# One kernel, two ways to feed the argument matmuls: pairs of 64-row matmuls in halves of the array, or single 128-row matmuls against a moving table padded with zeros

## The chip, the core and the metric

The kernel runs on one core of a Trainium2 chip. The metric is the device time of one execution in microseconds (us). The median of the three runs of the kernel before is 384.66 us (382.64 to 384.88). One further execution was recorded by the profiler; the profile, its chain of waits and all the durations quoted here come from that one.

## What is computed

Two branches read the same input `x` (2048 positions, 640 channels, bf16) and are mixed by a gate:

```
g = sigmoid((x * gate_w).sum(-1))
a = attention(x): 32 heads of 20, each position sees 8 keys at distances 0,2,..,14; then @ wo
b = long convolution of x with K, by FFT of length 4096;  K[d,l] = Re sum_n C[d,n]*dt*B[d,n]*exp(dt*A[d,n]*l)
out = g*a + (1-g)*(b + x*Dskip)
```

The change lies in the making of the convolution kernel K: 640 channels, 192 complex states each, 2048 positions.

## The kernel before

The work falls into four stretches. Up to about 40 us the inputs are loaded and the 12 parameter pieces for each channel and state are worked out on VectorE and ScalarE and stored to DRAM (`SSMParams`, tensor `Sprm`). From 24 to about 140 us TensorE does the QKV projection (L328, tile `tb`). From about 55 to 300 us it does the attention in eight slices of 256 positions: logits (L383, with L403 and L411 for the softmax), the weighted sum of the values (L447) and the output projection (L464). K is made between 73 and 267 us, woven in among these; the first FFT step follows (L1195), and from 301 us on the rest of the FFT convolution (`fft_conv`).

K is made by `KGen` in ten chunks `c`. A chunk has 64 channels: 8 in each of 2 halves of each of 4 groups. It goes through these steps:

- `load_L` issues eight small DMAs from SP. They bring the chunk's parameter pieces from `Sprm` into `L`, a tile of 128 rows. Rows 0 to 63 and rows 64 to 127 each hold a separate set (two rows of ones and 48 rows of pieces). There are two such tiles, used in turn, and a chunk's loads wait for the argument matmuls of two chunks before.
- The arguments. For each of three state tiles `u` and two kinds (0: the sine's argument, 304 columns; 1: the exponent's, 2 x 216 columns) a task of TensorE multiplies `L` (stationary) with the constant table `R` (moving) into a PSUM tile `ar`. A chunk has 12 tasks of kind 0 and 6 of kind 1, so there are 120 and 60 in all. For `u` below 2 a task of kind 0 is two matmuls, a task of kind 1 four; each uses 64 rows and 128 columns of the array (line L768), and the two that differ in `g2` sit in the two halves of its rows. For `u` = 2 the states left over from two halves of channels share a tile: each matmul becomes two of 64 rows and 64 columns (L773), four in the four quarters of the array.
- ScalarE turns each `ar` into sines (L785) or exponentials (L787). `ar` has two buffers, so TensorE can be at most two tasks ahead of ScalarE.
- VectorE multiplies sines and exponentials (`products`, L808 to L810).
- `kmm` sums over the states with 256 small matmuls a chunk (L826, 22 columns each): 128 rows by 32 columns of the array for `u` below 2, and 64 by 32 for `u` = 2, where two halves of channels share the rows. VectorE evicts the sum (L1179).

All these tasks, with those of the attention and the first FFT step, are given to a planner (`Plan`). Each has a duration, a due time and its engines; `Plan.order` lists them in a fixed order, and `emit` chains every engine's instructions in that order. So each engine works strictly in the planned order, and a task that waits holds up all that stands behind it on its engine. An argument task is planned at 0.15, 0.15 and 0.30 us (kind 0, `u` = 0, 1, 2) or 0.22, 0.22 and 0.40 us (kind 1), a quarter of a `kmm` at 0.18 or, for `u` = 2, 0.35 us.

Of the kernel before, what the change touches and what calls it, by code (L numbers as in the profile page):

```python
# [14 lines left out]
BF16 = mybir.dt.bfloat16  # L15
I16 = mybir.dt.int16
NPBF = ml_dtypes.bfloat16
# [19 lines left out]
def _attn_consts():  # L37
# [5 lines left out]
    for wp in range(W):  # L43
# [7 lines left out]
            v=[-164.3, -448.6, 45.4, 323.3, 710.0, 789.4, 646.8, 1095.8], g=[10.7, 292.0, -348.6, -469.5, -539.5, 427.8, 247.2, -1193.3, -158.0, -278.7, -66.5],  # L51
# [443 lines left out]
NST = 192  # L495
# [7 lines left out]
NPC = 12  # L503
KI = 32
MS = list(range(8)) + [258, 260, 262, 516, 772, 256, 512, 768, 1024, 1280, 1536, 1792, 2048, 2048]
NM = len(MS)
FIRST = 13
SW = 4 * (KI + 2 * NM)
EW = 4 * (KI + NM)
# [4 lines left out]
def _arg_consts():  # L514


    i = np.arange(KI)
    m = np.array(MS)
    sp = np.zeros((64, 4, KI), np.float32)
    sq = np.zeros((64, 4, 2, NM), np.float32)  # L520
    ep = np.zeros((64, 4, KI), np.float32)
    eq = np.zeros((64, 4, NM), np.float32)
    for qq in range(4):
        r = 2 + qq * NPC
        for j in range(3):
            sp[r + j, qq] = 8.0 * i - 124.0
            sq[r + j, qq] = (m % 256)[None]
            sq[r + 5 + j, qq] = (m // 256)[None]
        for j in range(2):
            ep[r + 3 + j, qq] = 8.0 * i  # L530
            eq[r + 3 + j, qq] = m
            sq[r + 8 + j, qq] = 1.0
            eq[r + 10 + j, qq] = 0.5
    sp[0] = MAGIC; sq[0] = MAGIC
    sp[1] = 8192.0
    sq[1, :, 0] = 24576.0
    sq[1, :, 1] = 8192.0
    rr = np.concatenate([np.concatenate([p, q.reshape(64, 4, -1)], axis=2).reshape(64, -1) for p, q in ((sp, sq), (ep, eq))], axis=1)
    return np.concatenate([rr, rr], axis=0).astype(NPBF)


def _shift_consts():
# [166 lines left out]
class KGen:  # L709
    def __init__(self, cst, pre, tc, prm):  # L710
        self.tc, self.nc, self.prm = tc, tc.nc, prm
        nc = tc.nc
        self.Lb = []
        for i in range(2):
            L = pre.tile([128, 2, 2, 2 * NST], BF16, name=f"L{i}", tag="PHI", bufs=3)
            nc.gpsimd.memset(L[:], 0.0)
            for g2 in range(2):
                nc.gpsimd.memset(L[64 * g2:64 * g2 + 2], 1.0)
            self.Lb.append(L)
        self.R = cst.tile([128, SW + EW], BF16, name="Rarg")  # L720
        nc.gpsimd.dma_start(self.R[:], nc.inline_tensor(_arg_consts(), name="c_rarg").ap())
        self.S12 = cst.tile([128, 2, 128], BF16, name="S12")
        nc.gpsimd.dma_start(self.S12[:], nc.inline_tensor(_shift_consts(), name="c_s12").ap())
# [10 lines left out]
    def load_L(self, c):  # L734
        nc = self.nc
        L = self.Lb[c % 2]
        for g in range(4):
            for v in range(2):
                d0 = 160 * g + 80 * v + 8 * c
                src = self.prm.S[d0:d0 + 8].rearrange("(s q) i n -> (q i) s n", q=4)  # L740
                nc.sync.dma_start(L[64 * (g % 2) + 2:64 * (g % 2) + 2 + 4 * NPC, g // 2, :, NST * v:NST * v + NST], src)

    def plan(self, pl, pa, pk, start, hold, params, opened, fin):
        nc, R = self.nc, self.R
# [4 lines left out]
        for c in range(NCH):  # L749
            d0, dd = start(c), start(c + 1) - start(c)  # L750
            L = self.Lb[c % 2]
# [4 lines left out]
            for kind in (0, 1) if c % 2 == 0 else (1, 0):  # L756
                for u in range(3):
                    ends[u, kind] = []
                    for gp in range(2):
                        for sub in range(2) if kind == 0 else (None,):  # L760
                            def args(_, u=u, kind=kind, gp=gp, sub=sub, b=b, L=L):
                                ar = b["ar"] = pa.tile([128, 2, 512], F32, name="ar")
                                for sb, a0 in ((sub, 0),) if kind == 0 else ((0, 0), (1, EW)):
                                    c0, ncol = ((0, SW), (SW, EW))[kind]
                                    for g2 in range(2):
                                        rows = slice(64 * g2, 64 * g2 + 64)
                                        if u < 2:
                                            nc.tensor.matmul(ar[:, g2, a0:a0 + ncol], L[rows, gp, sb, NST * u:NST * u + 128], R[rows, c0:c0 + ncol],  # L768
                                                             start=True, stop=True, tile_position=(64 * g2, 0))
                                        else:  # L770
                                            m0 = NST * gp + 128
                                            for h in range(2):
                                                nc.tensor.matmul(ar[64 * h:64 * h + 64, g2, a0:a0 + ncol], L[rows, h, sb, m0:m0 + 64], R[rows, c0:c0 + ncol],  # L773
                                                                 start=True, stop=True, tile_position=(64 * g2, 64 * h))
                                b["ar", u, kind, gp, sub] = ar

                            def act(_, u=u, kind=kind, gp=gp, sub=sub, b=b):
                                opened()
                                ar = b.pop(("ar", u, kind, gp, sub))
                                if gp == 0 and not sub:  # L780
                                    b["T", u, kind] = self.ring[kind][self.turn[kind] % len(self.ring[kind])]
                                    self.turn[kind] += 1
                                dst = b["T", u, kind]
                                if kind == 0:
                                    nc.scalar.activation(dst[:, 2 * gp:2 * gp + 2, sub, :], ar[:].bitcast(I16)[:, :, 0:2 * SW:2], ACT.Sin, scale=SCL)  # L785
                                else:
                                    nc.scalar.activation(dst[:, 2 * gp:2 * gp + 2].rearrange("p g s n -> p g (s n)"), ar[:, :, 0:2 * EW], ACT.Exp)  # L787
                            due = d0 + dd * k / 18.0
                            first = not ends[u, kind]
                            a = pl.add(f"arg{c}{kind}{u}{gp}{sub}", "P", ((0.15, 0.15, 0.30), (0.22, 0.22, 0.40))[kind][u], args, deps=[Lt], after=[prevarg] + ([self.moved] if c == HC + 2 else []), acq=["ar"],  # L790
                                       due=due - pr["argl"], eq=(304, 432)[kind])
                            t = pl.add(f"act{c}{kind}{u}{gp}{sub}", "A", (0.62, 0.83)[kind], act, deps=[a], after=[prevact] + (hold if first and kind == 0 and ns == NTR - 1 else []), acq=[("trg", "exq")[kind]] if first else [],
                                       rel=[("ar", a)], due=due, table=("sin", "exp")[kind])
                            if first:
                                held[u, kind] = t
                                ns += kind == 0
                            prevarg, prevact = a, t
                            argt[c].append(a)
                            ends[u, kind].append(t)
                            k += kind + 1  # L800
            for u in range(3):
# [12 lines left out]
                def kmm(_, u=u, b=b, j=0):  # L814
                    if u == 0 and j == 0:
                        b["kps"] = pk.tile([128, 2, 256], F32, name="kps", tag="kb")
                    pt, qq = b["pq", u]
                    kps, started = b["kps"], b["started"]
                    for ql in (2 * j, 2 * j + 1):
                        for v in range(2):  # L820
                            for c2 in ((u,) if u < 2 else (0, 1)):
                                for g in range(4):
                                    r0 = 0 if u < 2 else 64 * (g // 2)
                                    rows = slice(0, 128) if u < 2 else slice(r0, r0 + 64)
                                    k = 8 * (g if u < 2 else 2 * c2 + g % 2) + ql
                                    nc.tensor.matmul(kps[32 * g:32 * g + 32, c2, NM * ql:NM * ql + NM],  # L826
                                                     pt[rows, k, v, :], qq[rows, k, v, :],
                                                     start=(g not in started), stop=(u == 2 and v == 1), skip_group_check=True,
                                                     tile_position=(r0, 32 * g))
                                    started.add(g)  # L830
                due = d0 + dd * (0.55 + 0.16 * u) + pr["dl"][c]
# [442 lines left out]
```

## Time and profile before

| of the profiled execution | |
|---|---|
| its own time | 384.76 us |
| span from the first to the last instruction | 383.0 us |
| granted TensorE clock, mean | 0.950 |
| argument matmuls L768, from 73.4 to 253.8 us | 320, 37.0 us busy |
| argument matmuls L773, from 82.4 to 257.0 us | 320, 19.6 us busy |
| state sums L826, from 105.3 to 266.6 us | 2560, 30.2 us busy |
| sines L785 (both buffers) and exponentials L787 on ScalarE | 59.6 + 15.1 and 50.2 us |
| products L808, L809 and L810 on VectorE (largest groups) | 16.5, 16.5 and 21.3 us |

A row of the profile gives the engine, the line, what is written from what, the shape, the count, and after the bar the busy time and the mean duration of one. A matmul's duration runs from its start to its modelled end and holds some 0.17 us in which its last columns pass through the array; the next matmul may start inside it. The distance between starts therefore tells what a matmul costs TensorE. PE is TensorE, PEld its weight loads, DVE is VectorE, ACT is ScalarE, POOL is GpSimd. PEclk is the granted TensorE clock as a share of full speed. The chain is the list of steps, each released by the one ahead of it, that ends with the last instruction.

### The profile page before, as it was taken

The page shows a single profiled execution, that of the slowest core. Times are in us where ns is not written, and L with a number is a line of the kernel's source. Part 1 is how long each engine was busy: PE and PEld are TensorE (multiplying, and loading weights), DVE is VectorE, ACT ScalarE, POOL GpSimd, SP SyncE. Part 2 cuts the span into 40 slices and gives each one's busy share as a digit, 9 for nine tenths or more (in the row PEclk, how much of TensorE's full clock was granted, in tenths as well). Part 3 has the DMA queues.
Part 4 walks back from the last instruction along what each step waited for, and adds up shares of the span by engine and source line. Part 5 has one row for each costly group of instructions (what it writes and reads, how often), then busy time and mean ns, then how long its engine had stood idle before and what let it go on. Part 6 is the DMA issues. An engine that isn't in the chain of part 4 may idle for free.

```text
span 383.0 us, 11863 instructions
## 1 busy us (share of the span) xinstructions
PE 316.9 (83%) x5102; PEld 191.0 (50%) x5126; DVE 323.0 (84%) x437; ACT 304.1 (79%) x427; POOL 89.3 (23%) x122
## 2 busy tenths in 40 slices
PE   0268999998999979988997699889999899987760
PEld 0144564433445545444454344557777655656760
DVE  4879997669999989889998799999896389999782
ACT  1699884677979889789879698988987798995890
POOL 8930331140211001513653100100010022000053
PEclk9998999999999999999989757999999999998996
DMA  8982878472645233686455850403740199926056
GB/s 266 373 252 94 246 212 256 117 215 86 193 125 157 64 112 95 158 224 188 104 124 134 274 154 2 151 2 101 254 140 34 36 211 244 207 40 222 2 119 159
DMA packets 51529, 58.84 MB, mean 154 GB/s; under 512 B 36244, under 2 KB 43284, under 8 KB 51220
## 3 DMA queue, kind: packets, MB, share of 16 engines
q1 hardware_dynamic: 41492, 28.78, 28.3%
q0 software_dynamic: 8256, 28.69, 25.6%
q8 instruction: 40, 0.66, 0.7%
q10 hardware_dynamic: 1728, 0.61, 0.7%
q14 instruction: 13, 0.11, 0.1%
HBM read 38.29 MB, written 19.77 MB: 152 GB/s over the span
## 4 chain that ended last, share of the span: by engine, by line
PE 51%; ACT 19%; DVE 13%; DMA 9%; issue 5%; SPq 1%; POOL 1%; POOLq 0%; ACTq 0%; DVEq 0%
PE tb L328 13%; PE tb L447 7%; PE ar L768 6%; PE fp L1024 5%; PE tb L464 5%; PE kps L826 4%; PE bp L1195 3%; DMA aim<-in_B_A_im_dram 3%; ACT big L787 3%; ACT sp_u L1027 3%; ACT big L785 3%; PE lg L383 3%; DVE bufA L985 3%; ACT sp_k L1027 3%; PE ar L773 2%
## 5 line engine op out<-in xcount | busy, mean ns | idle before, releaser
L328 PE MATMUL tb<-bufA 128*128 128x512 bf16 x283 | 71.5, 388 | 6.5 <-DVE bufA L492 2.1
L785 ACT ACTIVATE big<-ar 128x608 bf16<-128x608 int16 x96 | 59.6, 677 | 10.2 <-PE ar L768 9.4
L787 ACT ACTIVATE big<-ar 128x864 bf16<-128x864 f32 x60 | 50.2, 897 | 4.1 <-PE ar L768 3.3
L442 DVE TENSOR_TENSOR pv<-vc,asb 128x2048 bf16<-128x2048 bf16 x40 | 47.2, 1219 | 4.3 <-PE tb L447 2.1
L328 PEld LDWEIGHTS <-bufA 128*128 128x128 bf16 x300 | 33.2, 120 | 35.1 <-issue 12.2
L377 DVE TENSOR_TENSOR prod<-qc,kc 128x2048 bf16<-128x2048 bf16 x40 | 47.9, 1219 | 2.7 <-PE lg L383 2.5
L768 PE MATMUL ar<-Rarg,L 64*128 64x304 bf16 (+1 forms) x320 | 37.0, 290 | 5.8 <-ACT big L785 2.4
L447 PE MATMUL tb<-pv,ident 128*128 128x512 bf16 (+1 forms) x185 | 39.1, 348 | 2.5 <-DVE prj L492 1.0
L826 PE MATMUL kps<-qq,pt 128*32 128x22 bf16 (+1 forms) x2560 | 30.2, 175 | 4.6 <-issue 4.2
L1024 PEld LDWEIGHTS <-PHI 128*128 128x128 bf16 x256 | 24.8, 97 | 17.6 <-issue 7.4
L826 PEld LDWEIGHTS <-pt 128*32 128x32 bf16 (+1 forms) x2560 | 23.3, 93 | 17.5 <-issue 12.3
L464 PE MATMUL tb<-wo_sb,oT 128*128 128x320 bf16 x160 | 27.7, 310 | 0.0
L768 PEld LDWEIGHTS <-L 64*128 64x128 bf16 x320 | 13.7, 94 | 27.7 <-issue 25.3
L447 PEld LDWEIGHTS <-ident 128*128 128x128 bf16 x192 | 17.8, 99 | 17.3 <-issue 5.5
L490 ACT ACTIVATE prj<-tb 128x512 bf16<-128x512 f32 x28 | 16.5, 598 | 10.9 <-PE tb L328 9.9
L959 POOL DMA_DIRECT2D PHI<-c_phi x8 | 4.5, 558 | 79.5 <-PE fp L1024 41.7
L773 PE MATMUL ar<-Rarg,L 64*64 64x304 bf16 (+1 forms) x320 | 19.6, 298 | 3.8 <-ACT big L787 1.6
L1027 ACT ACTIVATE sp_k<-fp 128x1280 bf16<-128x1280 f32 x16 | 19.1, 1236 | 3.3 <-PE fp L1024 3.0
L810 DVE TENSOR_TENSOR qq<-big 128x1408 bf16<-128x1408 bf16 x24 | 21.3, 886 | 0.0
L1024 PE MATMUL fp<-bufA,PHI 128*128 128x320 bf16 x128 | 19.1, 298 | 2.3 <-ACT sp_u L1027 1.5
L243 PE MATMUL ar<-ident,xn 128*128 128x128 bf16 x80 | 7.9, 263 | 15.6 <-DMA xn<-in_A_x_dram 14.1
L1024 PE MATMUL fp<-big,PHI 128*128 128x320 bf16 x128 | 19.2, 298 | 1.8 <-ACT sp_k L1027 1.8
(201 smaller groups left out, 633.0 us busy)
## 6 DMA issues: line engine op xcount, KB each, us to landing
asb<-aS SPq DMA_DIRECT2D x8, 512.0 KB, 4.0
PSI<-c_psi SPq DMA_DIRECT2D x8, 512.0 KB, 10.2
PHI<-c_phi POOLq DMA_DIRECT2D x8, 384.0 KB, 6.6
Sprm<-pc SPq DMA_DIRECT2D x12, 240.0 KB, 3.7
L<-Sprm SPq DMA_DIRECT2D x80, 36.0 KB, 2.6
kc<-kS POOLq DMA_DIRECT2D x8, 337.5 KB, 4.7
vc<-vS POOLq DMA_DIRECT2D x8, 337.5 KB, 4.9
xn<-in_A_x_dram SPq DMA_DIRECT2D x4, 640.0 KB, 12.4
```

The lines of the kernel that those rows point to most:

```text
L328: nc.tensor.matmul(ppf, self.wq[:, kt, which * D + e:(which + 1) * D:5], self.xT[:, c0 // 1024, kt, c0 % 1024:c0 % 1024 + SC], start=(kt = ...
L377: nc.vector.tensor_tensor(b[e][:], b["qc"][:, e, :].unsqueeze(1).to_broadcast([128, W, C]), win(b["kc"][:, e, :], 0, W, DIL, C), ALU.mult)
L442: nc.vector.tensor_tensor(b["pv", e][:, :, k, :].rearrange("p w (b t) -> p w b t", t=64), for_e, aw, ALU.mult)
L447: nc.tensor.matmul(b["op", e][:, 0:n, :], ident[:], b["pv", e][:, w, 0:n, :], start=(w == 0), stop=(w == W - 1))
L464: nc.tensor.matmul(apf[:, :320], b["oT"][:, e, i * 128:(i + 1) * 128], wo_sb[:, e, hf * 320:(hf + 1) * 320], start=(e == 0), stop=(e == 4))
L768: nc.tensor.matmul(ar[:, g2, a0:a0 + ncol], L[rows, gp, sb, NST * u:NST * u + 128], R[rows, c0:c0 + ncol], start=True, stop=True, tile_pos ...
L773: nc.tensor.matmul(ar[64 * h:64 * h + 64, g2, a0:a0 + ncol], L[rows, h, sb, m0:m0 + 64], R[rows, c0:c0 + ncol], start=True, stop=True, til ...
L785: nc.scalar.activation(dst[:, 2 * gp:2 * gp + 2, sub, :], ar[:].bitcast(I16)[:, :, 0:2 * SW:2], ACT.Sin, scale=SCL)
L787: nc.scalar.activation(dst[:, 2 * gp:2 * gp + 2].rearrange("p g s n -> p g (s n)"), ar[:, :, 0:2 * EW], ACT.Exp)
L826: nc.tensor.matmul(kps[32 * g:32 * g + 32, c2, NM * ql:NM * ql + NM], pt[rows, k, v, :], qq[rows, k, v, :], start=(g not in started), stop ...
L1024: nc.tensor.matmul(fp[:, fl, 0:320].rearrange("p (c x) -> p c x", x=32), PHI[:, fl, kind, :], B[:, :, 2 * f1 + ri].rearrange("p c q g -> p ...
L1027: nc.scalar.activation(t[:], fp[:, :, 0:320].rearrange("p f (x g) -> p x f g", g=4), ACT.Identity)
```

## The change

The table `R` is stored twice: once with zeros in rows 64 to 127, once with zeros in rows 0 to 63. Each argument matmul takes all 128 rows of `L` and picks the copy of `R` that has zeros where the other set of rows lies. It no longer names a place in the array. The three state tiles are cut differently out of 384 columns of `L` (two times 192 states): tiles 0 and 2 each belong to one half of the channels, tile 1 holds 64 states of each. Every argument task of kind 0 is then two matmuls of 128 by 128 with 304 columns, every one of kind 1 four with 216. In `kmm` it is now tile 1 that is done in 64-row matmuls and tile 2 in 128-row ones. `load_L` still issues eight DMAs of the same size, in another order and to other columns. The planner's durations and due times are as before.

```diff
@@ _arg_consts
-    return np.concatenate([rr, rr], axis=0).astype(NPBF)
+    z = np.zeros_like(rr)
+    return np.stack([np.concatenate([rr, z], axis=0), np.concatenate([z, rr], axis=0)], axis=1).astype(NPBF)
@@ KGen.__init__
-        self.R = cst.tile([128, SW + EW], BF16, name="Rarg")
+        self.R = cst.tile([128, 2, SW + EW], BF16, name="Rarg")
@@ KGen.load_L
-        for g in range(4):
+        for g in range(2):
             for v in range(2):
-                d0 = 160 * g + 80 * v + 8 * c
-                src = self.prm.S[d0:d0 + 8].rearrange("(s q) i n -> (q i) s n", q=4)
-                nc.sync.dma_start(L[64 * (g % 2) + 2:64 * (g % 2) + 2 + 4 * NPC, g // 2, :, NST * v:NST * v + NST], src)
+                for h in range(2):
+                    d0 = 160 * ((2 * v + g + 2 * h) % 4) + 80 * h + 8 * c
+                    src = self.prm.S[d0:d0 + 8].rearrange("(s q) i n -> (q i) s n", q=4)
+                    l0 = NST * (h ^ v)
+                    nc.sync.dma_start(L[64 * g + 2:64 * g + 2 + 4 * NPC, :, v, l0:l0 + NST], src)
@@ KGen.plan, args
                                     for g2 in range(2):
-                                        rows = slice(64 * g2, 64 * g2 + 64)
-                                        if u < 2:
-                                            nc.tensor.matmul(ar[:, g2, a0:a0 + ncol], L[rows, gp, sb, NST * u:NST * u + 128], R[rows, c0:c0 + ncol],
-                                                             start=True, stop=True, tile_position=(64 * g2, 0))
-                                        else:
-                                            m0 = NST * gp + 128
-                                            for h in range(2):
-                                                nc.tensor.matmul(ar[64 * h:64 * h + 64, g2, a0:a0 + ncol], L[rows, h, sb, m0:m0 + 64], R[rows, c0:c0 + ncol],
-                                                                 start=True, stop=True, tile_position=(64 * g2, 64 * h))
+                                        l0 = 128 * (2 - u if gp else u)
+                                        nc.tensor.matmul(ar[:, g2, a0:a0 + ncol], L[:, sb, gp, l0:l0 + 128], R[:, g2, c0:c0 + ncol],
+                                                         start=True, stop=True)
@@ KGen.plan, kmm
-                            for c2 in ((u,) if u < 2 else (0, 1)):
+                            for h in (0, 1) if u == 1 else (u // 2,):
                                 for g in range(4):
-                                    r0 = 0 if u < 2 else 64 * (g // 2)
-                                    rows = slice(0, 128) if u < 2 else slice(r0, r0 + 64)
-                                    k = 8 * (g if u < 2 else 2 * c2 + g % 2) + ql
-                                    nc.tensor.matmul(kps[32 * g:32 * g + 32, c2, NM * ql:NM * ql + NM],
+                                    r0 = 64 * (g // 2) if u == 1 else 0
+                                    rows = slice(r0, r0 + 64) if u == 1 else slice(0, 128)
+                                    k = 8 * ((g + 2 * h) % 4) + ql
+                                    nc.tensor.matmul(kps[32 * g:32 * g + 32, h, NM * ql:NM * ql + NM],
                                                      pt[rows, k, v, :], qq[rows, k, v, :],
-                                                     start=(g not in started), stop=(u == 2 and v == 1), skip_group_check=True,
+                                                     start=(g not in started), stop=(v == 1 and u == 1 + h), skip_group_check=True,
                                                      tile_position=(r0, 32 * g))
```

## The prediction

> **What bounds the kernel now.** I read the page first (sections 1, 2 and 4), then the groups by shape, the timeline of TensorE, the stretches of 5 us, and last the chain of waits piece by piece from 70 to 260 us, where the changed matmuls lie.
>
> ```profile
> PE 316.9 (83%) x5102; PEld 191.0 (50%) x5126; DVE 323.0 (84%) x437; ACT 304.1 (79%) x427; POOL 89.3 (23%) x122
> ...
> PEclk9998999999999999999989757999999999998996
> ...
> PE 51%; ACT 19%; DVE 13%; DMA 9%; issue 5%; SPq 1%; POOL 1%; POOLq 0%; ACTq 0%; DVEq 0%
> ```
>
> Three engines are busy about four fifths of the span, but the chain lies on PE for half of it, and the clock falls in one place, behind the middle. The groups by shape give the rows of the matmuls that change:
>
> ```profile
> L768 PE MATMUL ar<-Rarg,L 64*128 64x304 bf16 x160 | 23.8, 319 | 4.2 <-ACT big L785 2.4 <-ACT bufA L785 1.2
> L768 PE MATMUL ar<-Rarg,L 64*128 64x216 bf16 x160 | 13.2, 261 | 1.6 <-ACT big L787 1.0 <-DVE nxt L492 0.4
> L773 PE MATMUL ar<-Rarg,L 64*64 64x304 bf16 x160 | 12.5, 334 | 1.6 <-ACT big L785 1.1
> ```
>
> These means hold the pass through the array, so I price by the distance between starts (timeline of PE; start, duration of the run, count):
>
> ```profile
> 102.65 1.27 PE L328 MATMUL tb<-bufA 128*128 128x512 bf16 x5
> 103.86 0.30 PE L768 MATMUL ar<-Rarg,L 64*128 64x304 bf16 x2
> 104.09 1.27 PE L328 MATMUL tb<-bufA 128*128 128x512 bf16 x5
> ...
> 108.47 0.43 PE L768 MATMUL ar<-Rarg,L 64*128 64x304 bf16 x4
> ...
> 110.48 0.32 PE L773 MATMUL ar<-Rarg,L 64*64 64x304 bf16 x4
> ```
>
> Two of 64x304 take 0.30 us and four take 0.43: a second pair adds 0.13, what one such matmul needs alone, so the two of a pair run side by side. Four quarter matmuls take 0.32 us, so all four run side by side. And each change of shape costs a pause: five L328 stream for 5 x 0.2175 = 1.09 us (eight of L447 take 1.74 us on the chain), from 102.65 to 103.74, yet L768 starts at 103.86; its 0.13 us are over at 103.99, and L328 starts at 104.09. That is 0.12 and 0.10 us. Between runs of one shape the starts follow without such a pause. I use 0.10 us.
>
> The stretches (length, then busy us and count of PE, PEld, DVE, ACT, POOL; clock; DMA share; GB/s):
>
> ```profile
> 125.00:130.00 5.00, 4.30 (x148) 2.63 (x150) 4.80 (x8) 4.76 (x7) 0.00 (x0) 1.00 0.03 7
> ...
> 210.00:215.00 5.00, 3.13 (x148) 1.97 (x147) 4.83 (x6) 4.07 (x5) 0.00 (x0) 1.00 1.02 331
> 215.00:220.00 5.00, 3.66 (x83) 1.38 (x84) 2.43 (x4) 2.75 (x5) 1.68 (x3) 0.50 0.60 211
> 220.00:225.00 5.00, 4.69 (x108) 2.25 (x107) 5.00 (x7) 4.67 (x8) 0.00 (x0) 0.50 0.90 269
> 225.00:230.00 5.00, 4.88 (x148) 2.29 (x150) 4.93 (x9) 4.68 (x8) 0.00 (x0) 0.50 0.24 47
> ```
>
> From 110 us on PE, DVE and ACT are close to full together. From 215 to 235 us PE runs at half clock, and even so DVE and ACT are full from 220 us on. The chain, piece by piece:
>
> ```profile
> 212.69 0.57 PE kps L826 x63
> 213.26 2.61 issue
> 215.88 0.41 PE kps L826 x21
> ...
> 222.22 0.82 PE ar L773 x7
> ```
>
> At 213.26 PE stands 2.61 us for nothing the profile shows, with the DMA engines full (1.02); then the clock halves.
>
> **The change, part by part.**
>
> *More streaming.* Every task now takes twice its time on PE. A task of kind 0 goes from 0.13 to 0.26 us, with any `u`, since four quarters took 0.13 as well. A task of kind 1 goes from two pairs of 216 (2 x 0.09: eight take 0.54, four 0.36) to four, 0.18 to 0.36. So 120 x 0.13 + 60 x 0.18 = 15.6 + 10.8 = +26.4 us of PE.
>
> *Fewer changes of shape.* I counted along both programs' instruction orders, which agree run by run. Before, 305 neighbours on PE differ in shape, after 196: the arguments now have the shape of L328, L447, L464, L403 and L411, while beside L826 and L383 (32 columns) the pause stays. 109 x 0.10 = -10.9 us. PE net: +15.5 us at full clock.
>
> *What of it lies on the path.* In the chain from 70 to 215 us I counted 168 matmuls of L768 and 120 of L773. A matmul of L768 adds 0.13/2 or 0.18/4, in the mean 0.054 us; one of L773 0.13/4 or 0.18/8, in the mean 0.027. So 168 x 0.054 + 120 x 0.027 = +12.3 us. On the chain 57 ends of argument runs touch a run of 128x128 on PE: -5.7. From 235 to 260 us there are 24 of L768 and 5 ends: +1.3 - 0.5 = +0.8. A chain stays a path when its pieces grow, so +7.4 us is a floor for these stretches, +15.5 the ceiling where PE bounds throughout. What was off the chain grows too and can come to end last; for that I add 1.5, about a fifth of the room between.
>
> *The clock.* [...] I count columns times the share of the array that a matmul covers, in spans of 3.4 us. The span ahead of 215 us has some 2,080 of 8,190 (five L464 with 1,600, a pair of L768 with 304, 63 of L826 with 173), and 1,700 to 2,400 follow in the five at half clock; the one ahead of the half clock at 198 us has 1,880. Spans with over 3,000 are followed by full clock. An argument task counts double afterwards, 900 to 1,500 more in each of the five, so the clock should come back after one span.
>
> [...]
>
> What a full clock gives back: 14.9 us of the chain from 215 to 235 us are PE; about 3 of them are pauses, which do not shrink (a pair takes 0.37 us from start to start at half clock, 0.25 of it streaming), so at most (14.9 - 3)/2 = 6 us, and at least nothing, as DVE and ACT are busy 17.2 and 17.0 us of the 20. Against it stand the arguments there, 25 x 0.054 + 19 x 0.027 - 0.2 = +1.7. DVE is the nearest limit: 20 - 17.2 = 2.8 us can go at most, so I take -1.5 net for the stretch, with ends -4.3 and +1.7. The half clock at 198 us: ends 0 and -1.6, taken -0.5.
>
> *Small parts.* `R` doubles from 130 to 260 KB. It is issued at 13.4 us on POOL's queue, when 350 GB/s move: 0 to 0.4 us on the load of `A_im`, which the chain passes until 15.7; taken 0.1, as most of that load is in by then. `load_L` keeps eight DMAs on SP, but the first task's pieces come first and fifth instead of first and third: two issues of 0.42 us, 0.8 at most; taken 0, because the loads run a chunk ahead and PE waited 0.6 us for them in all. `kmm` keeps 256 matmuls a chunk; the 64-row ones move to tile 1 and the last quarters halve from 32 to 16. Those took 0.30 and 0.20 us to the next start, so 0.1 less at ten ends and 0.1 more ten times in the middle: 0, ends -1 and +1. The orders of DVE, ACT, POOL and SP are the same, and no wait is added but those for the pieces of `L`.
>
> *Sum.* 7.4 + 1.5 - 1.5 - 0.5 + 0.1 = +7.0 us. The profiled execution took 384.76 us, 0.1 over the median of 384.66. So 391.7 us, 1.8% over the median.
>
> **Rivals.**
>
> *The arguments are hidden.* DVE and ACT are full from 110 us on, `ar` lets PE run two tasks ahead, and PE has idle time there (4.30 us busy of 5 from 125 us on). Then only the stretch from 70 to 110 us pays, where PE is busy 38.3 of 40 us and the chain gives 3.1 - 1.4 = +1.7, less the clock's 2: 384.5 us. Against it: the chain runs over PE for 37.8 of the 50 us from 110 to 160.
>
> *PE becomes the bound throughout.* All +15.5 count and the clock gives nothing: 400.2 us. [...] For it: all engines follow one order, and a late task holds up all behind it. Against it: PE's idle pieces.
>
> *Faster than before.* The pause at 213.26 goes, since PE has 320 instructions fewer and its stand falls outside the full DMA queues, and with it the half clock behind it: -2.6 - 6 - 1.6 against +7.4: 382.0 us. It ends faster only where the stretch from 213 to 235 us shrinks by more than 7.4 us. Against it: DVE and ACT allow 2.8 us beside the pause.
>
> *No added streaming.* That pairs did not run side by side before, so that nothing is added, is excluded by 0.30 against 0.43 us.
>
> [...]
>
> **How the numbers follow.** The forecast (388.5 to 396) 0.50, hidden 0.25, PE-bound or clock unmoved 0.15, faster than before 0.10. The range reaches from the hidden case to the PE-bound one, 384 to 400 us, with the case ahead of it and a tail left out. A measurement of this kernel tells about 1% (3.8 us) from no change. Slower by over 1% are the forecast and the PE-bound case, 0.65; the hidden case lies within 1%, and of the 0.10 I give it 0.03: 0.28; faster by over 1% 0.07.
>
> **What would show it.** PE's matmuls of 128x304 start 0.13 us apart, with no pause beside L328; 480 argument matmuls stand where 640 were. The chain from 70 to 215 us is 7 to 8 us longer. PEclk shows at most two short dips from 195 to 240 us. It is wrong if ACT waits no longer for `ar` than now (9.4 us at L785, 3.3 at L787), or if the stand of 2.6 us moves and multiplies.

## The result, and the profile after

The kernel after takes 389.45 us in the median (389.09 to 390.04), beside 384.77 us (382.64 to 385.44) for the kernel before on the same chip: a ratio of 1.0133, with a 95% interval of 1.0091 to 1.0174. It is 4.7 us slower, where +7.0 was forecast. The profiled execution took 389.49 us with a span of 387.7 us; before it was 384.76 and 383.0, again 4.7 apart. Where medians of two kernels are subtracted below, executions over 1.5% slower than the fastest of the same kernel are left out. The mean granted clock is 0.971, before 0.950.

The page of the kernel after (busy time and counts, the clock by slices, the chain by engine):

```profile
PE 330.3 (85%) x4966; PEld 213.8 (55%) x4966; DVE 322.6 (83%) x437; ACT 306.5 (79%) x427; POOL 89.8 (23%) x122
...
PEclk9999999999999999999999789999999999998986
...
PE 48%; ACT 20%; DVE 14%; DMA 8%; issue 5%; POOL 2%; SPq 0%; POOLq 0%; ACTq 0%; DVEq 0%
```

PE is busier by 13 us, DVE as busy as before and ACT by 2.4 us more. Behind the middle the clock still dips in one place, for a shorter time. The groups by shape of the kernel after have two rows of argument matmuls in place of four:

```profile
L770 PE MATMUL ar<-Rarg,L 128*128 128x304 bf16 x240 | 48.2, 298 | 4.3 <-ACT big L782 1.8 <-ACT bufA L782 0.8
L770 PE MATMUL ar<-Rarg,L 128*128 128x216 bf16 x240 | 29.7, 256 | 2.2 <-ACT big L784 0.9 <-DMA L<-Sprm 0.4
```

The waits of the kernel after (engine and line, whom it waited for, us in total, times, longest) show that ScalarE waits longer for the arguments, 12.3 and 4.8 us where it was 9.4 and 3.3:

```profile
ACT big L782 <- PE ar L770: 12.3, 19, 2.9
...
ACT big L784 <- PE ar L770: 4.8, 10, 0.9
```

The timeline of TensorE in the kernel after, at the place that the prediction priced (start, duration of the run, count):

```profile
103.44 0.42 PE L770 MATMUL ar<-Rarg,L 128*128 128x304 bf16 x2
103.70 1.24 PE L328 MATMUL tb<-bufA 128*128 128x512 bf16 x5
104.78 0.42 PE L770 MATMUL ar<-Rarg,L 128*128 128x304 bf16 x2
105.04 1.24 PE L328 MATMUL tb<-bufA 128*128 128x512 bf16 x5
106.21 0.27 PE L823 MATMUL kps<-qq,pt 128*32 128x22 bf16 x16
106.41 0.43 PE L770 MATMUL ar<-Rarg,L 128*128 128x304 bf16 x2
106.78 0.37 PE L823 MATMUL kps<-qq,pt 128*32 128x22 bf16 x32
```

From 103.44 to 103.70 two argument matmuls take 0.26 us, 0.13 each. Five L328 take 1.08 us from 103.70 to 104.78, and the next argument follows at once: the pause is gone. Beside L823 it stays: from 106.41 to 106.78 are 0.37 us, 0.26 and some 0.10.

Since DVE and ACT run the same instructions in the same order in both kernels, I took the start of each in the one trace from its start in the other. This lag says where the time went:

| time in the kernel before, us | after minus before, us |
|---|---|
| 69 | -0.2 |
| 125 | +2.2 |
| 163 | +3.8 |
| 168 to 209 (for a moment, at 200, 5.1) | +3.9 |
| 219 to 230 | +6.4 to +6.7 |
| 252 to 291 | +5.3 |
| last product | +5.4 to +5.7 |
| end of the span | +4.7 |

So nearly all that stays is lost between 70 and 163 us. From 209 to 230 some 2.6 us more are lost and then half given back; the last output transfers give back 0.7 to 1.0. The stretches of the kernel after behind 210 us (length, then busy us and count of PE, PEld, DVE, ACT, POOL; clock; DMA share; GB/s):

```profile
215.00:220.00 5.00, 2.00 (x100) 1.12 (x89) 2.37 (x3) 2.60 (x3) 0.00 (x0) 0.86 0.88 300
220.00:225.00 5.00, 5.00 (x85) 2.00 (x83) 2.59 (x4) 2.03 (x3) 1.69 (x3) 0.50 0.65 152
225.00:230.00 5.00, 4.22 (x87) 2.00 (x84) 4.85 (x8) 4.58 (x8) 0.00 (x0) 0.96 0.72 267
230.00:235.00 5.00, 4.85 (x180) 2.48 (x179) 5.00 (x7) 4.98 (x9) 0.00 (x0) 1.00 0.26 59
```

The chain of the kernel after in that place (start, length, what):

```profile
215.60 0.47 PE kps L823 x51
216.07 3.00 issue
219.07 0.27 PE kps L823 x12
219.34 0.55 PE lg L383 x4
219.89 0.62 PE ar L770 x2
220.51 1.33 PE tb L464 x5
221.84 0.48 PE kps L823 x32
222.32 0.62 PE ar L770 x2
```

PE stands again for nothing that the profile shows, 3.00 us (before 2.61), and the clock halves again, 0.5 us before the stand ends (before 0.9), but from 218.6 to 225.4 us only (before from 215.0 to 235.4). While it lasts, an argument task costs 0.62 us, where a pair took 0.37 us at half clock before, and five L464, which ran at full clock ahead of the stand before, cost 1.33 us. At 0.50 PE is busy 5.00 of 5 us; of the 3.4 us ahead of 218.6 it stood for 2.5. The length of 3.4 us is that of the shortest stretch at one clock in both traces (3.413, in the kernel before from 197.9 to 201.3 us); the half clock here lasts twice as long (6.83), before six times (20.48).

### The profile page after: what moved, and what is told of

It reads as the page before. It is cut to its first block, busy times and chain, and to the rows that moved or that the text cites. A ratio compares the mean times of both kernels' runs of the same rounds, so it can differ in the third digit from the quotient of the medians.

```text
span 387.7 us, 11596 instructions
## 1 busy us (share of the span) xinstructions
PE 330.3 (85%) x4966; PEld 213.8 (55%) x4966; DVE 322.6 (83%) x437; ACT 306.5 (79%) x427; POOL 89.8 (23%) x122
## 4 chain that ended last, share of the span: by engine, by line
PE 48%; ACT 20%; DVE 14%; DMA 8%; issue 5%; POOL 2%; SPq 0%; POOLq 0%; ACTq 0%; DVEq 0%
PE ar L770 10%; PE tb L328 9%; PE tb L447 7%; PE fp L1021 5%; PE bp L1192 4%; ACT big L782 4%; PE tb L464 4%; PE kps L823 4%; ACT big L784 3%; ACT sp_u L1024 3%; DVE bufA L982 3%; ACT sp_k L1024 3%; PE lg L383 2%; DMA vc<-vS 2%; DVE t L611 2%
## 5 line engine op out<-in xcount | busy, mean ns | idle before, releaser
L770 PE MATMUL ar<-Rarg,L 128*128 128x304 bf16 (+1 forms) x480 | 78.0, 277 | 6.5 <-ACT big L782 1.8
L328 PE MATMUL tb<-bufA 128*128 128x512 bf16 x300 | 74.0, 389 | 4.2 <-DVE bufA L492 1.9
L782 ACT ACTIVATE big<-ar 128x608 bf16<-128x608 int16 x96 | 61.0, 676 | 12.8 <-PE ar L770 12.3
L770 PEld LDWEIGHTS <-L 128*128 128x128 bf16 x480 | 41.9, 97 | 27.7 <-issue 14.1
L328 PEld LDWEIGHTS <-bufA 128*128 128x128 bf16 x300 | 34.0, 120 | 33.5 <-issue 11.1
L377 DVE TENSOR_TENSOR prod<-qc,kc 128x2048 bf16<-128x2048 bf16 x40 | 47.9, 1217 | 4.0 <-PE lg L383 3.9
L823 PEld LDWEIGHTS <-pt 128*32 128x32 bf16 (+1 forms) x2560 | 23.1, 92 | 20.6 <-issue 18.7
L823 PE MATMUL kps<-qq,pt 128*32 128x22 bf16 (+1 forms) x2560 | 29.8, 175 | 4.7 <-issue 4.7
L464 PE MATMUL tb<-wo_sb,oT 128*128 128x320 bf16 x160 | 27.0, 305 | 0.0
L490 ACT ACTIVATE prj<-tb 128x512 bf16<-128x512 f32 x28 | 16.5, 597 | 12.2 <-PE tb L328 11.6
L1024 ACT ACTIVATE sp_u<-fp 128x1280 bf16<-128x1280 f32 x16 | 19.2, 1237 | 1.8 <-PE fp L1021 1.8
```

What stands on the lines that cost most here:

```text
L328: nc.tensor.matmul(ppf, self.wq[:, kt, which * D + e:(which + 1) * D:5], self.xT[:, c0 // 1024, kt, c0 % 1024:c0 % 1024 + SC], start=(kt = ...
L377: nc.vector.tensor_tensor(b[e][:], b["qc"][:, e, :].unsqueeze(1).to_broadcast([128, W, C]), win(b["kc"][:, e, :], 0, W, DIL, C), ALU.mult)
L464: nc.tensor.matmul(apf[:, :320], b["oT"][:, e, i * 128:(i + 1) * 128], wo_sb[:, e, hf * 320:(hf + 1) * 320], start=(e == 0), stop=(e == 4))
L770: nc.tensor.matmul(ar[:, g2, a0:a0 + ncol], L[:, sb, gp, l0:l0 + 128], R[:, g2, c0:c0 + ncol], start=True, stop=True)
L823: nc.tensor.matmul(kps[32 * g:32 * g + 32, h, NM * ql:NM * ql + NM], pt[rows, k, v, :], qq[rows, k, v, :], start=(g not in started), stop= ...
L1024: nc.scalar.activation(t[:], fp[:, :, 0:320].rearrange("p f (x g) -> p x f g", g=4), ACT.Identity)
```

## The experiments

My first theory was that the kernel pays for the doubled streaming on PE, less the pauses saved, where PE lies on the path. The rivals: other engines hide it, so that it is paid only in places; or the time comes from something else that moved with it. During the runs a third came up, the stands of PE that the chain puts down to "issue". Each job ran the kernel before anew; its medians were 384.77, 386.28, 387.34 and 386.5 us, so times are compared inside a job or by the traces.

**e1_pairs: the new layout with the old pairs.** Tables, loads and `kmm` of the kernel after, but each matmul takes its 64 rows, so that two run side by side (the lines that change):

```diff
+rows = slice(64 * g2, 64 * g2 + 64)
-nc.tensor.matmul(ar[:, g2, a0:a0 + ncol], L[:, sb, gp, l0:l0 + 128], R[:, g2, c0:c0 + ncol],
-                 start=True, stop=True)
+nc.tensor.matmul(ar[:, g2, a0:a0 + ncol], L[rows, sb, gp, l0:l0 + 128], R[rows, g2, c0:c0 + ncol],
+                 start=True, stop=True, tile_position=(64 * g2, 0))
```

> The cut of the state tiles, the loads of L and the sums as in the changed kernel, but each argument matmul again takes 64 rows in its half of the array, so two run side by side; the third tile is two pairs of 64x128 instead of quarters. If doubled streaming is what costs (my theory): 26.4 us of PE streaming gone again, changes of shape about as before (some 10 fewer, since the quarters are gone: about -1 us of PE), so 383 to 385.5 us. If the new cut, the order of the loads or the moved 64-row sums cost (rival): near 389.

Measured: 392.12 us (389.07 to 394.41), ratio 1.0132 (1.0065 to 1.0198). Missed: a kernel with none of the added streaming is as slow as the one with it. By the lag it loses only 0.6 us from 69 to 163 us, but then stands and runs at half clock. Its timeline of TensorE, with the idle time ahead of a run and its cause in brackets, and its stretch from 195 to 245 us:

```profile
215.51 0.39 PE L383 MATMUL lg<-prod,ind 128*32 128x512 bf16 x2
220.85 0.61 PE L383 MATMUL lg<-prod,ind 128*32 128x512 bf16 x2 [4.95 <-issue]
```

```profile
195.00:245.00 50.00, 39.91 (x994) 20.05 (x994) 42.21 (x69) 40.16 (x59) 13.35 (x15) 0.76 0.48 130
```

The stand comes in the middle of four L383, so what stands is not a line or a kind of matmul. That is the clock of the kernel before in this stretch (0.76); the kernel after has 0.93:

```profile
195.00:245.00 50.00, 42.44 (x1066) 25.17 (x1058) 42.26 (x69) 41.65 (x61) 11.66 (x16) 0.93 0.47 133
```

**e2_twice: the pairs, each issued twice.** The doubled streaming without the saved changes of shape (the line that differs from e1):

```diff
-for g2 in range(2):
+for g2 in (0, 1, 0, 1):
```

> As e1, but every pair of argument matmuls is issued twice, the second over the first: the streaming of the changed kernel (0.26 and 0.36 us a task) with all the changes of shape kept. Theory (each change of shape costs 0.10 us and half of them lie on the path): 389.45 plus 4 to 6, so 393 to 396 us. Rival (the pauses lie beside other work, only streaming counts): 388.5 to 390.5. PE has 960 argument matmuls here, 320 more than before.

Measured: 400.05 us (398.87 to 403.23), ratio 1.0377 (1.0314 to 1.0439), above what was expected. Its timeline of TensorE at the place priced above:

```profile
104.52 0.43 PE L771 MATMUL ar<-Rarg,L 64*128 64x304 bf16 x4
104.88 1.27 PE L328 MATMUL tb<-bufA 128*128 128x512 bf16 x5
106.09 0.43 PE L771 MATMUL ar<-Rarg,L 64*128 64x304 bf16 x4
```

From one L771 to the next are 1.57 us; it is 1.34 in the kernel after and 1.44 in the one before. Against the kernel before, the lag grows by 9.7 us from 69 to 163 us in this kernel, by 0.6 in e1 and by 4.0 in the kernel after. So doubling the streaming costs 9.1 us there, and giving up the halves gives back 5.7. Of these, 0.9 and 1.3 us are stands (those of over half a us that are no wait, counted from the end of a matmul's streaming, which is some 0.2 us more than the idle time in the rows: 2.8 us in this stretch of e2, 1.9 in e1, 1.5 in the kernel after); 8.2 and 4.4 remain, beside 9.2 and 4.0 that the prediction's prices make of the chain's pieces there.

**e3_light_before and e4_light_after: less work on VectorE.** In both kernels 16 of the 40 products L377 are left out:

```diff
+if e % 2:
+    b[e] = b[e - 1]
+    return
```

> Kernel before, with 16 of the 40 products of the attention left out on VectorE (e = 1 and 3 read the product of e = 0 and 2): 16 x 1.22 = 19.5 us less on VectorE, everything else as it is. If VectorE bounds the stretch in which K is made: 5 to 12 us faster, 373 to 380. If TensorE bounds it: within 3 us of the kernel before, 382 to 385. To be compared with e4.

> Changed kernel with the same 16 products left out. Theory (the rest of the +15.5 us of TensorE hides under a full VectorE): with VectorE relieved the changed kernel loses more against its partner, e4 minus e3 = 7 to 12 us. Rival (what is lost is a fixed share of the chain on TensorE, or lost before VectorE fills): e4 minus e3 stays at 4 to 6 us.

Measured: 389.54 us (387.65 to 395.79) and 393.02 us (390.76 to 394.75), ratios 1.0093 (1.006 to 1.0126) and 1.0178 (1.0113 to 1.0243). Neither theory of e3 holds: with 10 us less of VectorE from 70 to 125 us (37.51 busy, before 47.65) the kernel is not faster. Its stands of over 0.6 us that are no wait add up to 7.6 us from 60 to 290 us, where the kernel before has 3.4 (e4 has 6.5), and one wait that grew from 1.8 us stands in its list of waits:

```profile
DVE pv L445 <- DMA asb<-aS: 3.8, 1, 3.8
```

The difference of the two is 3.6 us, not the 7 to 12 that would have shown VectorE to hide part of the added streaming, and below the 4 to 6 of its rival too. That theory falls.

**e5, e6, e7: the same programs, moved by 128 instructions of PE.** By then a pattern stood in the traces: the stands of PE of over 0.6 us that are no wait begin at the same place when PE's instructions are counted in blocks of 256. With its semaphore instructions counted, and a matmul for every weight load, this holds in the traces of all fourteen kernels of this document: for all 57 such stands between 60 and 290 us the count of instructions ahead, from the first in the trace, leaves 193 or 194 when it is divided by 256. The page counts the packets of a queue that it calls "instruction", first of the kernel before, then of the kernel after:

```profile
q8 instruction: 40, 0.66, 0.7%
```

```profile
q8 instruction: 39, 0.64, 0.7%
```

The trace of the kernel before has 5,126 weight loads and 5,102 matmuls (24 records are missing), some 10,250 instructions or 256 for each of the 40 packets, and 0.66 MB / 40 is 16.5 KB. For some stands I looked up when the block ahead was entered (128 matmuls back, each with its load), when the packet moved, and when PE ran on:

| kernel | block entered, us | packet, us | PE runs on, us |
|---|---|---|---|
| before | 133.8 | 135.0 | 137.50 |
| before | 193.3 | 194.6 | 196.98 |
| before | 210.4 | 213.6 | 215.88 |
| after | 213.8 | 216.85 | 219.07 |
| e1_pairs | 214.2 | 218.35 | 220.85 |
| e5 (below) | 250.6 | 253.2 | 255.62 |

From the packet to the next instruction are 2.2 to 2.5 us each time. From the entry to the packet are 1.2 to 1.3 us in the first two rows and 2.7 to 4.2 in the rest. The three longest, 3.0 to 4.2 us, lie where the DMA engines are full (a share of 1.01 to 1.04 in between), but load alone does not order the rest: the share is 0.89 and 0.53 in the first two rows and 0.84 in e5. From the entry to the next instruction after the stand are 3.7 us in the first two rows and 5.0 to 6.7 in the last four. That a block which PE uses up in less time leaves it standing is my estimate from these six rows; the dense L823 and L826 are that fast: 64 start in 0.6 us.

The test puts 64 matmuls of 10 columns (128 instructions with their loads) into a scratch tile at the start, when PE waits for `x`:

```diff
+for _ in range(64):
+    nc.tensor.matmul(lt[:, 1, 0:10], lg10[:], ident[0:10, 0:10], start=True, stop=True)
```

e5 is the kernel before with them, e6 the kernel after, e7 is e1.

> Kernel before, with 64 matmuls of 10 columns more at its very start, where PE has nothing to do before 15 us. All later instructions of PE then lie 128 places further on. Theory (PE stands where it reaches an instruction block that has not been fetched: in the kernel before each stand of over 0.6 us lies at the same place, 187, of a block of 256 instructions): the stands lie at place 187 again, so 128 instructions earlier in the work, the one of 2.8 us at 213 us becomes shorter or longer, and the time moves by 1 to 5 us either way although the work is the same. Rival (the stands belong to the work at these points, its data or waits): they stay at the same matmuls, and the time stays within 1 us.

> Changed kernel with the same 64 matmuls at its start. Theory: the stand of 3.2 us at 216 us moves 128 instructions forward in the work, up to 165 us the kernel runs within 0.7 us as without them (the 4 us of lag that it has there come from streaming), behind it the time moves by 1 to 5 us. Rival: no change beyond 1 us.

> e1 with the same 64 matmuls at its start. Theory: e1 was slow because of its stands (5.3 us at 216, 1.9 at 250, 1.2 at 180 us) and not because of its loads or sums; they move, and it comes down to 383 to 387 us, or at least its time up to 163 us stays within 1 us of the kernel before. Rival (the new cut of the tiles costs): it stays at 390 to 392 us.

Measured: 396.90 us (395.06 to 401.5), 396.62 us (395.53 to 400.6) and 395.69 us (390.67 to 399.88); ratios 1.0228 (1.0161 to 1.0296), 1.0256 (1.0177 to 1.0334) and 1.0249 (1.0159 to 1.0339). The added matmuls run from 2.7 to 4.4 us, as the line's answer in the trace of e5 says (minimum, median and maximum in ns, first and last start):

```profile
L586 PE MATMUL ar<-ident,lg x64: 163/163/163, 2.7 to 4.4; 10*128 10x10 bf16 x64
```

All three came out above what was expected of them, or lost more on the way: e5 moved by 9.6 us where 1 to 5 were expected, e7 did not come down to 383 to 387 us, and e6, which was to run like the kernel after up to 165 us, loses 6.8 us against it from 69 to 163 us. By the lag e5 is level with the kernel before until 125 us (0.1) and falls behind where stands now come, as in its timeline of TensorE:

```profile
252.87 0.21 PE L828 MATMUL kps<-qq,pt 64*32 64x22 bf16 x7
255.62 0.62 PE L828 MATMUL kps<-qq,pt 64*32 64x22 bf16 x57 [2.54 <-issue]
```

So 1.8 us of work in idle time cost the kernel before 9.6 us, more than the change did. The stands of over 0.6 us that are no wait, from 60 to 290 us by the rows' idle time, add up to 3.4 us in the kernel before and 11.7 in e5, 4.4 in the kernel after and 9.6 in e6, 9.4 in e1 and 10.8 in e7. And between the shifted kernels, e6 and e5, the medians differ by -0.1 us instead of +4.7. By the lag e6 is still 7.6 us behind e5 at 163 us and has most of that back by the end: from 215 to 300 us e5 has stands of 2.51, 1.50 and 2.54 us and 30.7 us at half clock, e6 of 2.42, 1.01 and 1.10 and half clock at 257 us only.

**e8_whole78: the whole array only where the clock falls.** e1 with the padded table in chunks 7 and 8 alone (against e1, shortened):

```diff
+WHOLE = (7, 8)
-rows = slice(64 * g2, 64 * g2 + 64)
+rows = slice(0, 128) if c in WHOLE else slice(64 * g2, 64 * g2 + 64)
-    tile_position=(64 * g2, 0)
+    tile_position=(0 if c in WHOLE else 64 * g2, 0)
```

> As e1, with the whole array and the padded table only in chunks 7 and 8, where the clock falls to half in the kernel before. Theory (there the doubled count of the array brings the clock back, and the added streaming hides behind VectorE and ScalarE): at most 7 us at half clock between 195 and 245 us, where e1 had 27; up to 205 us like e1; 3 to 6 us less than e1, 385 to 388 us, if the stands stay as long as in e1. Rival (streaming costs there too): as e1 or up to 3 us above it, 390 to 394 us.

Measured: 388.85 us (386.59 to 394.16), ratio 1.0066 (1.0024 to 1.0109): near the expected range, but no gain on the kernel before. Half clock from 195 to 245 us shrinks from 24 us in e1 (27 with the dip at 181 us) to 6.8, the clock of the stretch from 0.76 to 0.93:

```profile
195.00:245.00 50.00, 41.00 (x1039) 23.41 (x1038) 42.86 (x69) 41.61 (x61) 13.99 (x16) 0.93 0.48 131
```

A stand of 3.7 us ahead of 217 us stays.

**e9_few_before and e10_few_after: half of `kmm`.** One of the two terms of K's sum is left out, so that 1280 small matmuls are issued instead of 2560:

```diff
-for v in range(2):
+for v in (0,):
```

> Kernel before, with half of the sums over the states left out (only v = 0): 1280 of the 2560 matmuls of L826 and 2560 of PE's 10254 instructions are gone, and a block of 256 instructions lasts longer. Theory (a block that PE uses up in under about 3.5 us, the time from entering one block to the next being there, makes it stand): the stands of over 0.6 us at block places, 5.2 us before, fall below 2 us in all; 372 to 380 us. Rival (the stands belong to the full DMA queues at 213 us, whatever the number of instructions): a stand of over 2 us stays there. To be compared with e10.

> Changed kernel with the same half of the sums left out. What the change costs when the stands are out of the way: e10 minus e9. If doubled streaming costs what it showed up to 165 us: +3 to +7 us. Rival (the 4.7 us came from the places of the stands): within 1.5 us of e9.

Measured: 377.07 us (376.16 to 377.65), ratio 0.9788 (0.9724 to 0.9851), and 381.76 us (377.9 to 388.62), ratio 0.9872 (0.9816 to 0.9928). In neither trace does PE stand over 0.6 us at the end of a block, as expected of e9. The stretch from 195 to 245 us, first of e9, then of e10:

```profile
195.00:245.00 50.00, 42.41 (x783) 21.51 (x780) 49.65 (x77) 47.60 (x67) 10.63 (x16) 0.83 0.53 149
```

```profile
195.00:245.00 50.00, 43.41 (x740) 26.22 (x727) 49.34 (x76) 48.35 (x68) 11.11 (x16) 1.00 0.53 149
```

DVE is busy 49.65 and 49.34 of 50 us, where it was 44.63 in the kernel before and 42.26 in the kernel after: in these two VectorE is the limit here. The medians differ by 2.9 us, the profiled spans by 1.6 (377.0 and 375.4), and by the lag 1.6 to 1.8 us are lost from 69 to 163 us. That lies between the two expectations, 3 to 7 us or within 1.5; e10 scatters over 10.7 us, so the size stays open.

**e11_place_after and e12_place_before: a reckoned place.** From the traces I reckoned where blocks would end for each number of added matmuls, and took 104 for the kernel after and 108 for the one before, which promised the shortest stands (the edit is that of e5 with these counts).

> Changed kernel with 104 of the small matmuls at its start, 208 instructions. From its trace I reckoned where blocks would begin at each place, and how far each then falls short of 3.5 us (5.5 us where the DMA queues are full): 7.7 us of stands without them, 16.6 with 128 instructions (e6), 5.2 with 208, the least. So 386 to 389.5 us. Rival (any instructions added at the start cost, as in e5 to e7): 392 us or more.

> Kernel before with 108 of the small matmuls, 216 instructions. The same reckoning from its trace: 6.8 us of stands without them, 14.5 with 128 (e5), 5.1 with 216, the least. So 382 to 386 us, and e11 minus e12 is 2 to 5 us. Rival (any instructions added at the start cost): 390 us or more.

Measured: 396.49 us (393.55 to 399.06) and 388.69 us (385.23 to 391.3), ratios 1.0292 (1.0206 to 1.0377) and 1.0086 (1.0041 to 1.0131): both missed, on the slow side. The stands of e11, counted from the end of the streaming, add up to 5.5 us, where 5.2 were reckoned, those of e12 to 7.9 instead of 5.1, so the blocks lie where they were reckoned at best in e11; the time did not follow. (One more of e11, 2.00 us at 222.5 us and at the same place of a block, is put down to a wait for VectorE that ended 0.3 us before PE ran on.) In e11's profile 3.2 us of the lag behind the kernel after are there at 33 us already, ahead of any dense `kmm`, in a part whose chain lies on the load of `x`. From 125 to 163 us 2.9 more are lost and then given back, and the last product is 3.2 us behind: in the profiled execution of 393.55 us the placing gained nothing and cost nothing. Why the others took up to 399.06 us is not shown.

No kernel that computes everything beat the kernel before.

## Why the prediction came out as it did

The direction, the path up to 163 us and the two main prices were right; the sum was 2.3 us too high, and that it came so near is in part luck, since terms of both signs cancel. Up to 209 us it had +7.6 where the lag grew by 4.1, from there to 260 us -0.7 where it grew by 1.4, and the last transfers gave back some 0.7 that it did not have.

*More streaming and fewer pauses, 70 to 163 us.* The start distances are those predicted: 0.13 us a matmul, no pause beside L328, 0.10 beside L823. Of its +12.3 - 5.7 the prediction has 9.2 - 4.0 = +5.2 in this stretch. The lag grew by 4.0, or 4.7 without the stands, which are 0.7 us shorter there than before (1.5 for 2.2). e2 and e1 show the terms apart, 8.2 and 4.4. In this layout of the program the step was right. Its sum does not hold in every layout: over the same work the lag of the kernel with the change grows by some 1.5 us in e4 against e3, 1.7 in e10 against e9, 6.7 in e6 against e5 and 5 to 6 in e11 against e12. The stands there differ too, 2.0 us in e3 and 0.5 in e4, 1.4 in e12 and 3.5 in e11, which accounts for a part of that.

*The floor of +7.4.* This failed, and with it the sign that the chain from 70 to 215 us would be 7 to 8 us longer, where the lag grew by 4.1: "A chain stays a path when its pieces grow" made a floor of sums over a chain that holds 8% of "issue" and waits on DMA, which are free to shrink. From 163 to 215 us it gave the other +1.4, and up to 209 us the lag grew by 0.1. In the other four pairs it does not keep growing there either: it falls by 1.3 to 2.0 us in three and grows by 0.4 in e10 against e9. PE is busy 40.6 of the 47 us from 165 to 212 in the kernel before (42.8 in the kernel after), and 52.4 of the 55 from 70 to 125: where PE has idle pieces, longer tasks can go into them. That a full VectorE hid them is not borne out by e3 and e4; which idle pieces took them up is not shown.

*Off the chain, +1.5.* Not seen: from 69 to 209 us the lag grew by 4.1 us in all, beside 6.6 + 1.5 forecast.

*The clock, -1.5 and -0.5.* The step that failed is the sign. The text took the clock to come back after one span; it did after two, 6.8 us. But the prediction left the stand ahead of it out of the sum, and that stand stayed (3.00 for 2.61 us); the half clock now falls on argument tasks that cost 0.25 us more each and on five L464 that ran at full clock before. So the lag grew by 2.7 us up to 225 us and fell by 1.3 up to 252 us, +1.4 in all, where the sum has -1.5 here and +0.8 from 235 to 260 us. That the clock counts the padding is borne out by these spans. (A full one would hold some 8,180 columns at full clock, an estimate from the starts in the kernel before, 0.2158 us apart with 512 columns and 0.1090 with 256.) I took every span of 3.4 us at half clock from 195 to 245 us in all fourteen traces and summed columns times share of the array, each matmul by the part of its streaming that falls into the span. With the zero rows, all 34 spans that half clock follows have at most 2,916, all 21 that full clock follows at least 2,945. Without them four of the 21, in the kernel after, e4, e8 and e11, would have 2,128 to 2,288, and up to 2,612 are followed by half clock. The first of the two spans here has 2,916 and includes the last 0.5 us of the stand, the second 3,040. What starts the half clock is less clear: by the same count e11 goes on at full clock after a span of 2,176, while e9 halves after one of 2,969, so the count of the prediction does not settle that. The short dip at 198 us is gone, as taken; the lag at 209 us is what it was at 190.

*Small parts.* Taken at +0.1 for the load of `R` and 0 for the others; the lag at 69 us is -0.2.

*The rivals.* "Hidden" failed, since ScalarE waits longer and the lag grows up to 163 us, beyond 110. "PE-bound" failed from 163 us on. "Faster than before" failed at its first condition: it had 2.6 us go because PE has 320 instructions fewer. PE does have that many fewer (5,126 weight loads became 4,966, and as many matmuls go), but all 57 stands lie at one place of a block, and one block still ends in dense `kmm` while the DMA engines are full (a share of 1.01).

What stays open is how much of the 4.7 us is the edit and how much the place of the blocks. Pairs of kernels that differ by the edit alone gave +4.7, +3.6 (e4 and e3), -0.1 (e6 and e5) and +2.9 (e10 and e9), and +8.0 with unlike shifts (e11 and e12). That the added streaming costs time from 70 to 163 us is shown by all five; its size there, 1.5 to 6.7 us, and the total belong to the layout of the program. Open as well are the input stage, which came up to 3 us later in some traces, and why the reckoned places did not pay.

## What to carry to other kernels

Before small matmuls are padded to the full array, price both sides by the distance of starts: here a pair of 304 columns that was split cost 0.13 us and each change of shape 0.10 us. A task alone between wide matmuls, which saves two changes, gained by that (1.34 for 1.44 us); over the program 26.4 us of streaming stood against 109 saved changes, 10.9 us. Count such sums as a gain or a loss only where the engine is full; here the lag grew by 0.1 us from 163 to 209 us, where PE was busy 39.9 of 46 us in the kernel before. In a program like this one, with 2560 tiny matmuls, run an edit at more than one place of the instruction blocks before a per cent is put down to the edit: here +4.7 us became -0.1 with both kernels moved by 128 instructions.

## What was not expected of the hardware

PE stood 0.6 to 4.9 us, with no wait, at one place in its count of instructions by 256, 57 times in fourteen traces. In the six cases looked up, the packet for the next block moved 1.2 to 4.2 us after the last was entered, and PE ran on 2.2 to 2.5 us after that, so 3.7 us after the entry in two and 5.0 to 6.7 in four. Added work of 1.8 us in an idle place moved these ends by 128 instructions and cost the kernel before 9.6 us.

With rows of zeros counted like rows of data, spans of 3.4 us at half clock with 2,945 or more (columns times share of the array; the columns are those streamed in the span) were followed by full clock and those up to 2,916 by half clock, in 55 spans of fourteen traces. Without the zero rows there is no such order: four spans of 2,128 to 2,288 were followed by full clock, others of up to 2,612 by half.
